# Attention and two expert layers on one core: both shared engines' work given to VectorE, the coarse attention regrouped, its v summed by DMA

## The chip, the cores and the metric

The kernel runs on 1 core of one Trainium2 chip. The metric is the device time of the whole program in microseconds (us). The kernel before takes 828.25 us in the median of 3 runs (823.25 to 828.64). The engines are PE (matrix products), DVE (VectorE), ACT (ScalarE) and POOL (GpSimd); SP issues the DMA transfers.

## The reference

For 4 batches, 8 heads, 576 positions and 64 columns, two attentions are added. The coarse one works on means of 4 neighbouring positions (144 of them): every position of a group gets its group's output. The local one lets a query see the keys less than 4 positions away. The sum passes two expert layers.

```
q_d, k_d, v_d = means over 4 neighbours          # 144 x 64 per head
out_up    = repeat(softmax(scale * q_d @ k_d.T) @ v_d, 4)
out_local = softmax(mask(scale * q @ k.T)) @ v   # |i - j| < 4
x = out_up + out_local                           # 2304 tokens x 512
x = ((x @ w1) * (x @ w2)) @ w3 @ w_out           # layer A, width 1024
x = max(x @ m1, x @ m2, x @ m3) @ m_out          # layer B, width 768
```

The weights are float64 in memory.

## The kernel before, in words

The core runs one stream of tasks per engine. The functions add tasks to a `Program` (`add`), each with its engine or engines, an estimate of its cost there, the tiles that it reads and writes, and for a DMA its size. `order` plans the tasks forwards and backwards six times, keeps the best plan, and writes the instructions out in its order; every engine then works through its own list in order and waits by semaphores. A task with two options (`either`: DVE or POOL) goes to the one that the planner thinks ends it first. So the cost table (lines 305 to 310) and the lags between engines (`AFTER`, `lag`) set the order.

The work, with the names that the profile shows:

- **Weights.** Each block of 128 x 1024 float64 words (`raw`) becomes float32 in five steps (`float32`, lines 358 to 364): one on ACT, then four on DVE, which this document calls a conversion. The conversions of `wo` and `w3t` give `wf` (12 blocks); w3 and w_out are then multiplied on PE into one matrix (`pw`, line 591, in two halves of 32 products each in the program, 64 in all; the trace shows each product as two matmuls). The 8 blocks of w1, w2 and the 12 of layer B give `cv`, and each is split into a high half (ACT, line 334) and a low half (`w`, an `either` task, line 336). A product in layer A or B is three matmuls on such halves (`mm3`, lines 341 to 343).
- **Coarse attention**, `down`, 16 pairs of heads (4 per batch; "head" below means such a pair). `qk` is loaded, copied into planes for the local attention (ACT, line 392), and summed in fours (lines 397 and 399, `either`). Scores `sp` on PE: 3 windows of 64 queries, six products (line 408); maximum (DVE, 418), exponentials with sums (ACT, 423), 4 x sum (POOL, 429), reciprocal (DVE, 431), multiplication (line 432, `either`), transposes `pp` (PE, 440), copies (ACT, 443), products with v `po` (PE, 456). v is loaded whole (`vr`, one buffer, line 387) and summed in fours by two additions (447 and 449, `either`).
- **Local attention**, `slab`, 12 slabs of 192 queries: scores `sq` (PE, 501), mask, maximum, exponential, sum and division on DVE and ACT (508 to 520), transposes `ptq` (526), products `poq` (543), sum with the coarse output (DVE, 552), split into halves `xt` (ACT 334, `either` 336).
- **Layers A and B**: 6 chunks of 384 tokens, two slabs each; `front` (products `pf` with x or `yt`, combined into `z` on DVE, line 620, split into `g`), `back` (products `py`). Layer A begins when both slabs of chunk 0 and its first weights are there. Its output goes through memory (`y_dram`, `y`) to layer B. All A and B products stand in one fixed chain on PE.

Memory for weights is 12 slots; `raw` blocks, `wf` and split weights take turns in them. Four of the eight PSUM banks hold the long sums, four take everything else.

Of the kernel before, what the change touches and what calls it, by code (L numbers as in the profile page):

```python
# [16 lines left out]
P = 128  # L17
# [84 lines left out]
class Program:  # L102
# [41 lines left out]
    def order(self, rounds=6):  # L144

        ts = self.tasks
        for t in ts:
            for d in t.deps:
                ts[d].nexts.append(t.n)
        for t in reversed(ts):  # L150
            t.late = min((ts[n].late - self.lag(t.options, n) for n in t.nexts), default=0.0)
            t.late -= min(c for _, c in t.options) + t.size / self.RATE
        best = None
        for _ in range(rounds):
            done, places = self.forward()
            end = max(t.end for _, _, t, _ in done)
            if best is None or end < best[0]:
                best = end, done, places
            self.backward(done)
        for x, slot in best[2]:  # L160
            x.slot = slot
        return [(t, e) for _, _, t, e in sorted(best[1], key=lambda d: d[:2])]

    def lag(self, options, n):

        (e, _), *more = options
        to = self.tasks[n].options
        return 0.0 if not more and len(to) == 1 and e == to[0][0] != "SP" else self.AFTER[e]

    def backward(self, done):  # L170
# [6 lines left out]
        for _ in ts:  # L177
# [16 lines left out]
            for d in t.deps:  # L194
                left[d] -= 1
                by[d] = min(by[d], t.late - self.lag([(on[d], 0)], n))
                if not left[d]:
                    can[on[d]].append(d)

    def forward(self):  # L200
# [26 lines left out]
        while len(done) < len(ts):  # L227
# [30 lines left out]
            t.end = end + self.AFTER[e]  # L258
# [5 lines left out]
            for m in t.nexts:  # L264
                left[m] -= 1
                ready[m] = max(ready[m], end + self.lag([(e, 0)], m))
                if not left[m]:
                    offer(ts[m])
# [4 lines left out]
def attention_moe_kernel(ctx, tc, q0, k0, v0, mask0, ql, kl, vl, mask, qkp, vp, w12, w3t, wo, m123, mo, out):  # L273
# [20 lines left out]
    tqr, kr, qr, vwr, vrr, vdr = ring("tq", 2), ring("k", 5), ring("q", 5), ring("vw", 2), ring("vr", 1), ring("vd", 2)  # L294
# [10 lines left out]
    act = lambda n: [("ACT", 0.19 + n * 0.00085)]  # L305
    dve = lambda n: [("DVE", 0.16 + n * 0.00104)]
    psum = lambda n: [("DVE", 0.15 + n * 0.00104)]
    quick = lambda n: [("DVE", 0.12 + n * 0.0006)]
    either = lambda n: [("DVE", 0.18 + n * 0.00115), ("POOL", 0.2 + n * 0.0024)]
# [71 lines left out]
    def down(b, hp):  # L381
# [4 lines left out]
        v = vrr.tile([KH, 2, 4 * P], F32, "vr")  # L386
        dma(lambda: v(), lambda: vp[rd, i].rearrange("r p n -> p r n"), [], [v], KH * 4096 * 2)
# [3 lines left out]
        for to, x in ((lambda: w()[:, :S], 0), (lambda: k()[:, W:W + S], GD)):  # L391
            prog.add(act(S), lambda e, to=to, x=x: e.copy(
# [3 lines left out]
        s, vd = qk, vdr.tile([KH, 2, P], F32, "vd")  # L396
# [5 lines left out]
        sp = bank("sp")  # L402

        def scores(e):
            for w in range(QT):
                for a in range(2):
                    h = slice(a * D, (a + 1) * D)
                    e.matmul(  # L408
                        sp()[h, w * GD:(w + 1) * GD], s()[h, w * QS:w * QS + D], s()[h, GD:2 * GD],
                        start=True, stop=True,  # L410
# [3 lines left out]
        ex = er.tile([P, QT, GD], F32, "e")  # L414
        prog.add(pe(0.9), scores, [s], [sp, ex])
        two = twor.tile([P, 2, QT], F32, "two")
        spv = lambda: sp()[:, :QT * GD].rearrange("p (t n) -> p t n", t=QT)
        prog.add(psum(QT * GD), lambda e: e.reduce_max(two()[:, 0], spv(), axis=AX.X), [sp], [two])
        prog.add(act(3), lambda e: e.mul(two()[:, 0], two()[:, 0], -SCALE / 16.0), [], [two])

        def exponentials(e):
            for w in range(QT):
                e.activation(
                    ex()[:, w, :], spv()[:, w, :], AF.Exp, bias=two()[:, 0, w:w + 1], scale=SCALE / 16.0,
                    accum_out=two()[:, 1, w:w + 1],
                )

        prog.add([("ACT", 1.75)], exponentials, [sp], [ex, two])
# [3 lines left out]
        prog.add(either(QT * GD), lambda e: e.tensor_tensor(  # L432
            ex(), ex(), view(two(), QT, [[1, QT], [0, GD]]), op=ALU.mult), [two], [ex])
        pt = dpr.tile([KH, 2, 2, QT, QW], F32, "dp")
        for part in range(2):
            pp = bank("pp")

            def transposed(e, part=part, pp=pp):
                for w in range(QT):
                    e.transpose(pp()[:KH, w * P:(w + 1) * P], ex()[:, w, part * KH:(part + 1) * KH], ident)  # L440

            prog.add(pe(0.4), transposed, [ex], [pp, (pt, part)])
            prog.add(act(288), lambda e, part=part, pp=pp: e.copy(
                pt()[:, part].rearrange("p a t n -> p t a n"),
                view(pp()[:KH, :], 0, [[P + QW - QS, QT], [D, 2], [1, QW]]),
            ), [pp], [(pt, part)])
        prog.add(either(4 * P), lambda e: e.tensor_tensor(
            v()[:, 0], v()[:, 0], v()[:, 1], op=ALU.add), [], [v])
        prog.add(either(2 * P), lambda e: e.tensor_tensor(
            vd().rearrange("p h n -> p (h n)"), v()[:, 0, :2 * P], v()[:, 0, 2 * P:], op=ALU.add), [v], [vd])  # L450
        po = bank("po")

        def values(e):
            for a in range(2):
                for k in range(2):
                    e.matmul(
                        po()[a * D:(a + 1) * D, :GD], vd()[:, k, a * D:(a + 1) * D],
                        pt()[:, k, a].rearrange("p t n -> p (t n)"), start=(k == 0), stop=(k == 1),
# [5 lines left out]
        prog.add(pe(0.7), values, [vd, pt], [po, (od, hp)])  # L464
# [4 lines left out]
    def slab(n, xt, at):  # L469
# [36 lines left out]
        prog.add(pe(2.4), scores, [x for hp in range(HP) for x in planes[b, hp]], [*sps, st])  # L506
# [56 lines left out]
    def weights_product():  # L563
# [20 lines left out]
        for half in range(2):  # L584
            os = [Tile(b, [P, 512], F32, "pw") for b in acc]
            for n in range(NF):
# [6 lines left out]
                prog.add(pe(3.5), product, [dw, do], os, chained=True)  # L593
# [235 lines left out]
```

## Time and profile before

| what | value |
|---|---|
| median of 3 runs | 828.25 us |
| the profiled execution, its own time | 827.7 us |
| its span (first to last instruction) | 825.9 us |
| PE busy | 771.5 us, 93% |
| DVE, ACT, POOL busy | 399.7, 274.9, 138.6 us |

The profile is of one execution. Busy is the time in which an engine has an instruction running; PE is nearly always busy after the first 145 us, so the shares over the span say little of the beginning. The chain of waits that ended last is 75% PE and 11% DVE. In the views a row gives a group of instructions (line, engine, operation, output<-inputs, shapes, count, busy us, mean ns, idle time before them and what ended it) or, in the timeline, one instruction or a run of equal ones with its start and length.

### The profile page before, as it was taken

The page shows a single profiled execution, that of the slowest core. Times are in us where ns is not written, and L with a number is a line of the kernel's source. Part 1 is how long each engine was busy: PE and PEld are TensorE (multiplying, and loading weights), DVE is VectorE, ACT ScalarE, POOL GpSimd, SP SyncE. Part 2 cuts the span into 40 slices and gives each one's busy share as a digit, 9 for nine tenths or more (in the row PEclk, how much of TensorE's full clock was granted, in tenths as well). Part 3 has the DMA queues.
Part 4 walks back from the last instruction along what each step waited for, and adds up shares of the span by engine and source line. Part 5 has one row for each costly group of instructions (what it writes and reads, how often), then busy time and mean ns, then how long its engine had stood idle before and what let it go on. Part 6 is the DMA issues. An engine that isn't in the chain of part 4 may idle for free.

```text
span 825.9 us, 16670 instructions
## 1 busy us (share of the span) xinstructions
PE 771.5 (93%) x7120; PEld 711.2 (86%) x7120; DVE 399.7 (48%) x614; ACT 274.9 (33%) x585; POOL 138.6 (17%) x176
## 2 busy tenths in 40 slices
PE   2879877998999999999998999999999999999997
PEld 0334446998999989999998999899999999999997
DVE  5978999924143274254324599972222131311211
ACT  4255574331234443363212355422121121121111
POOL 2213479500001012010001026520000000000000
PEclk9999976999999999999999999999999999999999
DMA  9786553012103232221202377112101001010001
GB/s 336 230 309 202 160 176 77 15 49 60 39 4 77 67 103 56 77 72 26 60 6 89 121 240 252 61 44 87 39 1 39 1 1 39 1 39 0 20 20 39
DMA packets 45482, 68.85 MB, mean 83 GB/s; under 512 B 20640, under 2 KB 29856, under 8 KB 45408
## 3 DMA queue, kind: packets, MB, share of 16 engines
q1 hardware_dynamic: 45408, 67.79, 25.7%
q8 instruction: 56, 0.92, 0.5%
q14 instruction: 18, 0.15, 0.1%
HBM read 58.33 MB, written 9.44 MB: 82 GB/s over the span
## 4 chain that ended last, share of the span: by engine, by line
PE 75%; DVE 11%; DMA 7%; issue 4%; ACT 1%; POOL 1%; SPq 1%; ACTq 0%; POOLq 0%; DVEq 0%
PE pf L341 16%; PE pf L343 15%; PE pf L342 15%; PE py L341 7%; PE py L342 6%; PE py L343 6%; PE poq L543 3%; DVE cv L362 3%; DMA qk<-qkp 2%; PE pw L591 2%; DVE cv L364 2%; DMA vr<-vp 2%; PE sq L501 1%; DVE cv L360 1%; PE sp L408 1%
## 5 line engine op out<-in xcount | busy, mean ns | idle before, releaser
L620 DVE TENSOR_TENSOR z<-pf,z 128x384 f32<-128x384 f32 x120 | 66.7, 556 | 287.5 <-PE pf L343 287.2
L341 PE MATMUL pf<-yt,w 128*128 128x384 f32 x432 | 146.0, 338 | 1.4 <-DVE z L620 1.4
L343 PE MATMUL pf<-yt,w 128*128 128x384 f32 x432 | 145.9, 338 | 0.0
L342 PE MATMUL pf<-yt,w 128*128 128x384 f32 x432 | 145.9, 338 | 0.0
L341 PE MATMUL pf<-xt,w 128*128 128x384 f32 x384 | 134.3, 350 | 1.9 <-issue 1.1
L342 PE MATMUL pf<-xt,w 128*128 128x384 f32 x384 | 132.0, 344 | 2.1 <-POOL xt L336 2.1
L343 PE MATMUL pf<-xt,w 128*128 128x384 f32 x384 | 131.6, 343 | 0.0
L618 ACT COPY z<-pf 128x384 f32<-128x384 f32 x84 | 40.2, 479 | 168.2 <-PE pf L343 168.2
L334 ACT CAST g<-z 128x384 fp32r<-128x384 f32 x84 | 43.1, 513 | 149.4 <-DVE z L620 149.3
L591 PE MATMUL pw<-wf 128*128 128x512 f32 x128 | 66.1, 669 | 24.9 <-DVE wf L364 22.6
L341 PEld LDWEIGHTS pf<-yt,w 128*128 128x128 f32 x432 | 81.1, 188 | 2.0 <-issue 1.7
L342 PEld LDWEIGHTS pf<-yt,w 128*128 128x128 f32 x432 | 81.1, 188 | 0.0
L343 PEld LDWEIGHTS pf<-yt,w 128*128 128x128 f32 x432 | 81.1, 188 | 0.0
L341 PEld LDWEIGHTS pf<-xt,w 128*128 128x128 f32 x384 | 73.9, 192 | 4.7 <-issue 2.7
L591 PEld LDWEIGHTS pw<-wf 128*128 128x128 f32 x128 | 26.6, 216 | 57.8 <-issue 32.4
L342 PEld LDWEIGHTS pf<-xt,w 128*128 128x128 f32 x384 | 73.8, 192 | 2.6 <-POOL xt L336 2.6
L343 PEld LDWEIGHTS pf<-xt,w 128*128 128x128 f32 x384 | 73.7, 192 | 0.0
L341 PE MATMUL py<-g,wp 128*128 128x384 f32 x192 | 67.1, 350 | 0.4 <-ACT o L649 0.4
L342 PE MATMUL py<-g,wp 128*128 128x384 f32 x192 | 64.8, 338 | 2.1 <-issue 2.1
L343 PE MATMUL py<-g,wp 128*128 128x384 f32 x192 | 64.9, 338 | 0.0
L336 DVE TENSOR_TENSOR g<-z,g 128x384 fp32r<-128x384 f32 x72 | 42.2, 587 | 33.3 <-ACT g L334 33.0
L341 PE MATMUL py<-g,w 128*128 128x384 f32 x144 | 48.9, 340 | 1.9 <-ACT o L649 1.9
(90 smaller groups left out, 1118.2 us busy)
## 6 DMA issues: line engine op xcount, KB each, us to landing
qk<-qkp SPq DMA_DIRECT2D x16, 576.0 KB
raw<-m SPq DMA_DIRECT2D x18, 512.0 KB
raw<-w3t SPq DMA_DIRECT2D x16, 512.0 KB
raw<-w SPq DMA_DIRECT2D x16, 512.0 KB
vr<-vp SPq DMA_DIRECT2D x16, 288.0 KB
y_dram<-o SPq DMA_DIRECT2D x48, 96.0 KB
y<-y_dram SPq DMA_DIRECT2D x16, 288.0 KB
out<-o SPq DMA_DIRECT2D x24, 192.0 KB
```

The source lines that it names most:

```text
L334: prog.add(act(n), lambda e: e.copy(hi(), src()), reads, [(writes, ("hi", id(hi)))])
L336: psum(n) if from_psum else either(n), lambda e: e.tensor_tensor(lo(), src(), hi().bitcast(F32), op=ALU.subtract),
L341: nc.tensor.matmul(o, wlo, xhi, start=first, stop=False)
L342: nc.tensor.matmul(o, whi, xlo, start=False, stop=False)
L343: nc.tensor.matmul(o, whi, xhi, start=False, stop=last)
L360: prog.add(quick(1024), lambda e: e.tensor_scalar(u(), u(), 3, 0x3FFFFFF8, op0=ALU.logical_shift_left, op1=ALU.bitwise_and), [], [cv])
L362: prog.add(dve(1024), lambda e: e.scalar_tensor_tensor(u(), high(), 0xC0000000, u(), op0=ALU.bitwise_and, op1=ALU.bitwise_or), [raw], [cv])
L364: prog.add(dve(1024), lambda e: e.scalar_tensor_tensor(u(), low(), 29, u(), op0=ALU.logical_shift_right, op1=ALU.bitwise_or), [raw], [cv])
L543: e.matmul(pos[u]()[a * D:(a + 1) * D, i * BQ:(i + 1) * BQ], vw()[h, a, i], pt().rearrange("p a n -> p (a n)")[h, c:c + BQ], start=True, s ...
L591: e.matmul(os[i](), w()[:, i * P:(i + 1) * P], o(), start=n == 0, stop=n == NF - 1)
L618: prog.add(act(T), lambda e, pp=pp: e.copy(z(), pp()[:, :T]), [pp], [z])
L620: prog.add(psum(T), lambda e, pp=pp: e.tensor_tensor(z(), pp()[:, :T], z(), op=ALU.mult if kind == "A" else ALU.max), [pp], [z])
```

## The change

- `either` and `psum` become the DVE cost: POOL is no option any more for the low halves, the sums of q and k, or anything else. POOL keeps small memsets and the 4 x sum.
- The coarse scores take two windows of 72 queries for each head of the pair (four products on 72 rows, in two banks) in place of three windows of 64. The maximum is two instructions of 72 x 288 in place of one of 128 x 432, the exponentials four in place of three, the transposes eight of 72 x 72 in place of six of 72 x 128.
- The multiplication by the reciprocal moves from DVE or POOL to ACT: four instructions of 72 x 144.
- v's sum: four transfers of 72 x 256 (72 KB) into one tile `vd`, the first by SP, three by POOL with `accum_op` add, each of which waits for the one before; the two additions and `vr` go. `vd` has three buffers in place of two.
- The planner's costs and lags are rewritten (a DMA that POOL issues counts SP's lag).

```diff
-            t.late = min((ts[n].late - self.lag(t.options, n) for n in t.nexts), default=0.0)
+            t.late = min((ts[n].late - self.lag(t, t.options, n) for n in t.nexts), default=0.0)
...
+        if task.size:
+            return self.AFTER["SP"]
...
-            t.end = end + self.AFTER[e]
+            t.end = end + self.AFTER["SP" if t.size else e]
...
-    tqr, kr, qr, vwr, vrr, vdr = ring("tq", 2), ring("k", 5), ring("q", 5), ring("vw", 2), ring("vr", 1), ring("vd", 2)
+    tqr, kr, qr, vwr, vdr = ring("tq", 2), ring("k", 5), ring("q", 5), ring("vw", 2), ring("vd", 3)
...
-    act = lambda n: [("ACT", 0.19 + n * 0.00085)]
+    act = lambda n: [("ACT", 0.14 + n * 0.00098)]
-    psum = lambda n: [("DVE", 0.15 + n * 0.00104)]
-    quick = lambda n: [("DVE", 0.12 + n * 0.0006)]
-    either = lambda n: [("DVE", 0.18 + n * 0.00115), ("POOL", 0.2 + n * 0.0024)]
+    psum = dve
+    quick = lambda n: [("DVE", 0.16 + n * 0.00052)]
+    either = dve
...
-        v = vrr.tile([KH, 2, 4 * P], F32, "vr")
-        dma(lambda: v(), lambda: vp[rd, i].rearrange("r p n -> p r n"), [], [v], KH * 4096 * 2)
+        vd = vdr.tile([KH, 2, P], F32, "vd")
+        for r in range(TG):
+            prog.add(
+                [("SP", 0.36) if r == 0 else ("POOL", 1.0)],
+                lambda e, r=r: e.dma_start(
+                    vd().rearrange("p h n -> p (h n)"), vp[rd, i, r // 2, :, r % 2 * 2 * P:(r % 2 + 1) * 2 * P],
+                    **({"accum_op": ALU.add} if r else {})),
+                [], [vd], size=KH * 1024)
         prog.add([("POOL", 0.12)], lambda e: e.memset(k()[:, :W], 0.0), [], [(k, 1)])
         prog.add([("POOL", 0.12)], lambda e: e.memset(k()[:, W + S:], 0.0), [], [(k, 2)])
         prog.add([("POOL", 0.12)], lambda e: e.memset(w()[:, S:], 0.0), [], [(w, 1)])
         for to, x in ((lambda: w()[:, :S], 0), (lambda: k()[:, W:W + S], GD)):
-            prog.add(act(S), lambda e, to=to, x=x: e.copy(
+            prog.add([("ACT", 1.23)], lambda e, to=to, x=x: e.copy(
                 to().rearrange("p (c g r) -> p c g r", c=NC, r=TG), view(qk(), x, [[1, NC], [NC, NJ * NG], [2 * GD, TG]])),
                 [qk], [(k if x else w, 0)])
-        s, vd = qk, vdr.tile([KH, 2, P], F32, "vd")
+        s = qk
         prog.add(either(4 * GD), lambda e: e.tensor_tensor(
             qk()[:, :4 * GD], qk()[:, :4 * GD], qk()[:, 4 * GD:], op=ALU.add), [], [qk])
         prog.add(either(2 * GD), lambda e: e.tensor_tensor(
             s()[:, :2 * GD], qk()[:, :2 * GD], qk()[:, 2 * GD:4 * GD], op=ALU.add), [], [s])
-        sp = bank("sp")
+        sps = [bank("sp") for _ in range(2)]
         def scores(e):
-            for w in range(QT):
+            for half in range(2):
                 for a in range(2):
                     h = slice(a * D, (a + 1) * D)
                     e.matmul(
-                        sp()[h, w * GD:(w + 1) * GD], s()[h, w * QS:w * QS + D], s()[h, GD:2 * GD],
-                        start=True, stop=True,
+                        sps[a]()[:KH, half * GD:(half + 1) * GD], s()[h, half * KH:(half + 1) * KH],
+                        s()[h, GD:2 * GD], start=True, stop=True,
                     )
-        ex = er.tile([P, QT, GD], F32, "e")
-        prog.add(pe(0.9), scores, [s], [sp, ex])
-        two = twor.tile([P, 2, QT], F32, "two")
-        spv = lambda: sp()[:, :QT * GD].rearrange("p (t n) -> p t n", t=QT)
-        prog.add(psum(QT * GD), lambda e: e.reduce_max(two()[:, 0], spv(), axis=AX.X), [sp], [two])
+        ex = er.tile([KH, 4, GD], F32, "e")
+        prog.add(pe(0.55), scores, [s], [*sps, ex])
+        two = twor.tile([KH, 2, 4], F32, "two")
+        for a in range(2):
+            prog.add(psum(2 * GD), lambda e, a=a: e.reduce_max(
+                two()[:, 0, 2 * a:2 * a + 2], sps[a]()[:KH, :2 * GD].rearrange("p (t n) -> p t n", t=2), axis=AX.X),
+                [sps[a]], [(two, a)])
         prog.add(act(3), lambda e: e.mul(two()[:, 0], two()[:, 0], -SCALE / 16.0), [], [two])
-        def exponentials(e):
-            for w in range(QT):
+        def exponentials(e, a):
+            for w in range(2 * a, 2 * a + 2):
                 e.activation(
-                    ex()[:, w, :], spv()[:, w, :], AF.Exp, bias=two()[:, 0, w:w + 1], scale=SCALE / 16.0,
-                    accum_out=two()[:, 1, w:w + 1],
+                    ex()[:, w, :], sps[a]()[:KH, w % 2 * GD:(w % 2 + 1) * GD], AF.Exp, bias=two()[:, 0, w:w + 1],
+                    scale=SCALE / 16.0, accum_out=two()[:, 1, w:w + 1],
                 )
-        prog.add([("ACT", 1.75)], exponentials, [sp], [ex, two])
+        for a in range(2):
+            prog.add([("ACT", 1.16)], lambda e, a=a: exponentials(e, a), [sps[a]], [ex, two])
         prog.add([("POOL", 0.25)], lambda e: e.tensor_scalar(
             two()[:, 1], two()[:, 1], 4.0, 4e-9, op0=ALU.mult, op1=ALU.add), [], [two])
         prog.add([("DVE", 0.17)], lambda e: e.reciprocal(two()[:, 1], two()[:, 1]), [], [two])
-        prog.add(either(QT * GD), lambda e: e.tensor_tensor(
-            ex(), ex(), view(two(), QT, [[1, QT], [0, GD]]), op=ALU.mult), [two], [ex])
-        pt = dpr.tile([KH, 2, 2, QT, QW], F32, "dp")
+        def normalise(e):
+            for w in range(4):
+                e.mul(ex()[:, w], ex()[:, w], two()[:, 1, w:w + 1])
+        prog.add([("ACT", 1.12)], normalise, [two], [ex])
+        pt = dpr.tile([KH, 2, 2, GD], F32, "dp")
         for part in range(2):
             pp = bank("pp")
             def transposed(e, part=part, pp=pp):
-                for w in range(QT):
-                    e.transpose(pp()[:KH, w * P:(w + 1) * P], ex()[:, w, part * KH:(part + 1) * KH], ident)
-            prog.add(pe(0.4), transposed, [ex], [pp, (pt, part)])
+                for w in range(4):
+                    e.transpose(pp()[:KH, w * KH:(w + 1) * KH], ex()[:, w, part * KH:(part + 1) * KH], ident[:KH, :KH])
+            prog.add(pe(0.35), transposed, [ex], [pp, (pt, part)])
             prog.add(act(288), lambda e, part=part, pp=pp: e.copy(
-                pt()[:, part].rearrange("p a t n -> p t a n"),
-                view(pp()[:KH, :], 0, [[P + QW - QS, QT], [D, 2], [1, QW]]),
-            ), [pp], [(pt, part)])
-        prog.add(either(4 * P), lambda e: e.tensor_tensor(
-            v()[:, 0], v()[:, 0], v()[:, 1], op=ALU.add), [], [v])
-        prog.add(either(2 * P), lambda e: e.tensor_tensor(
-            vd().rearrange("p h n -> p (h n)"), v()[:, 0, :2 * P], v()[:, 0, 2 * P:], op=ALU.add), [v], [vd])
+                pt()[:, part].rearrange("p a n -> p (a n)"), pp()[:KH, :2 * GD]), [pp], [(pt, part)])
         po = bank("po")
         def values(e):
...
-                        pt()[:, k, a].rearrange("p t n -> p (t n)"), start=(k == 0), stop=(k == 1),
+                        pt()[:, k, a], start=(k == 0), stop=(k == 1),
-        prog.add(pe(0.7), values, [vd, pt], [po, (od, hp)])
+        prog.add(pe(1.05), values, [vd, pt], [po, (od, hp)])
```

The planner makes a new order from this. On **DVE at the beginning of the program** (from the fifth `wf` block on; `two` is the coarse maximum and reciprocal) before:

```order
L418 TENSOR_REDUCE two<-sp 128x3
L364 SCALAR_TENSOR_TENSOR wf<-raw,wf 128x1024
L359 TENSOR_SCALAR wf<-wf 128x1024
L360 TENSOR_SCALAR wf<-wf 128x1024
L362 SCALAR_TENSOR_TENSOR wf<-raw,wf 128x1024
L431 RECIPROCAL two<-two 128x3
L364 SCALAR_TENSOR_TENSOR wf<-raw,wf 128x1024
L432 TENSOR_TENSOR e<-e,two 128x432
L449 TENSOR_TENSOR vd<-vr 72x256
L399 TENSOR_TENSOR qk<-qk 128x288
```

and now:

```order
L366 SCALAR_TENSOR_TENSOR wf<-raw,wf 128x1024
L405 TENSOR_TENSOR qk<-qk 128x576
L407 TENSOR_TENSOR qk<-qk 128x288
L366 SCALAR_TENSOR_TENSOR wf<-raw,wf 128x1024
L405 TENSOR_TENSOR qk<-qk 128x576
L407 TENSOR_TENSOR qk<-qk 128x288
L427 TENSOR_REDUCE two<-sp 72x2 x2
L361 TENSOR_SCALAR wf<-wf 128x1024
L362 TENSOR_SCALAR wf<-wf 128x1024
L364 SCALAR_TENSOR_TENSOR wf<-raw,wf 128x1024
L366 SCALAR_TENSOR_TENSOR wf<-raw,wf 128x1024
L443 RECIPROCAL two<-two 72x4
```

All sums of q and k now stand between the conversions on DVE; the multiplication (432) and the sum of v (449) are gone from it.

On **POOL after its first memsets** (numbers are buffers: `vd_155`, `vd_159`, `vd_161` belong to heads 1 to 3, `vd_526` and `vd_573` to heads 4 and 5) before:

```order
L397 TENSOR_TENSOR qk_145<-qk_145 128x576
L399 TENSOR_TENSOR qk_145<-qk_145 128x288
L429 TENSOR_SCALAR two_249<-two_249 128x3
L447 TENSOR_TENSOR vr_155<-vr_155 72x512
L397 TENSOR_TENSOR qk_153<-qk_153 128x576
L429 TENSOR_SCALAR two_325<-two_325 128x3
L432 TENSOR_TENSOR e_331<-e_331,two_325 128x432
```

and now, from the second head's `two` on:

```order
L441 TENSOR_SCALAR two_333<-two_333 72x4
L392 DMA vd_161<-vp 72x256
L392 DMA vd_155<-vp 72x256
L392 DMA vd_159<-vp 72x256
L392 DMA vd_161<-vp 72x256
L392 DMA vd_526<-vp 72x256
L441 TENSOR_SCALAR two_565<-two_565 72x4
L392 DMA vd_573<-vp 72x256
L392 DMA vd_526<-vp 72x256
L392 DMA vd_573<-vp 72x256
L392 DMA vd_526<-vp 72x256
```

The arithmetic is gone from POOL; accumulating transfers of two heads alternate in its list, and the second transfer of head 4 stands behind the first of head 5.

On **DVE where layer B's weights are converted** (`cv`, `w`) one block before:

```order
L620 TENSOR_TENSOR z<-pf,z 128x384
L359 TENSOR_SCALAR cv<-cv 128x1024
L336 TENSOR_TENSOR w<-cv,w 128x512
L360 TENSOR_SCALAR cv<-cv 128x1024
L362 SCALAR_TENSOR_TENSOR cv<-raw,cv 128x1024
L364 SCALAR_TENSOR_TENSOR cv<-raw,cv 128x1024
```

and now:

```order
L630 TENSOR_TENSOR z<-pf,z 128x384
L361 TENSOR_SCALAR cv<-cv 128x1024
L338 TENSOR_TENSOR w<-cv,w 128x512
L338 TENSOR_TENSOR g<-z,g 128x384
L338 TENSOR_TENSOR w<-cv,w 128x512
L362 TENSOR_SCALAR cv<-cv 128x1024
L364 SCALAR_TENSOR_TENSOR cv<-raw,cv 128x1024
L366 SCALAR_TENSOR_TENSOR cv<-raw,cv 128x1024
```

The second low half of each block and the low half of `g`, which POOL did in this stretch, stand on DVE.

## Rows read from the trace of the kernel before

**Rows 1.** The page's head, the engines' busy time, and DMA's busy tenths in 40 slices.

```profile
span 825.9 us, 16670 instructions
PE 771.5 (93%) x7120; PEld 711.2 (86%) x7120; DVE 399.7 (48%) x614; ACT 274.9 (33%) x585; POOL 138.6 (17%) x176
...
DMA  9786553012103232221202377112101001010001
```

**Rows 2.** Busy time by stretch (columns as its first line says, x instructions).

```profile
core 0: us, PE busy (x) PEld busy (x) DVE busy (x) ACT busy (x) POOL busy (x), PEclk, DMA share, GB/s
8.31:131.08 122.77, 93.25 (x1073) 49.87 (x1073) 110.44 (x132) 65.08 (x125) 51.04 (x51) 0.89 0.69 230
131.08:144.86 13.78, 11.58 (x48) 10.75 (x48) 13.64 (x14) 7.02 (x11) 11.71 (x8) 0.71 0.24 50
144.86:466.00 321.14, 315.12 (x4009) 300.89 (x4010) 134.72 (x263) 108.59 (x255) 35.52 (x58) 0.99 0.19 55
468.25:545.67 77.42, 73.72 (x414) 72.21 (x413) 72.34 (x76) 38.50 (x69) 33.89 (x23) 1.00 0.54 178
545.67:825.90 280.23, 275.57 (x1568) 275.24 (x1566) 68.56 (x132) 51.64 (x123) 2.73 (x4) 1.00 0.07 24
```

**Rows 3.** DVE timeline, a conversion while POOL is idle.

```profile
8.31 0.69 DVE L359 TENSOR_SCALAR wf<-wf 128x1024 f32<-128x1024 f32 x1 [8.31 <-ACT wf L358]
9.04 0.69 DVE L360 TENSOR_SCALAR wf<-wf 128x1024 uint32<-128x1024 uint32 x1
9.77 1.22 DVE L362 SCALAR_TENSOR_TENSOR wf<-raw,wf 128x1024 uint32<-128x1024 uint32 x1
11.03 1.23 DVE L364 SCALAR_TENSOR_TENSOR wf<-raw,wf 128x1024 uint32<-128x1024 uint32 x1
```

**Rows 4.** Timeline of POOL and DVE, two instructions that overlap.

```profile
19.09 1.48 POOL L397 TENSOR_TENSOR qk<-qk 128x576 f32<-128x576 f32 x1 [14.12 <-ACT k L392]
...
19.34 1.79 DVE L360 TENSOR_SCALAR wf<-wf 128x1024 uint32<-128x1024 uint32 x1
```

**Rows 5.** Groups by line and shape over the whole span.

```profile
L336 DVE TENSOR_TENSOR wp<-pw,wp 128x512 fp32r<-128x512 f32 x8 | 5.1, 674 | 0.0
...
L397 DVE TENSOR_TENSOR qk<-qk 128x576 f32<-128x576 f32 x9 | 6.8, 758 | 11.4 <-ACT k L392 11.4
...
L418 DVE TENSOR_REDUCE two<-sp 128x3 f32<-128x432 f32 x16 | 9.7, 603 | 14.9 <-PE sp L408 14.8
...
L508 DVE TENSOR_TENSOR s<-sq,masks 128x256 f32<-128x256 f32 x24 | 9.1, 416 | 13.2 <-PE sq L501 13.2
...
L423 ACT ACTIVATE e<-sp,two 128x144 f32<-128x144 f32 x48 | 17.7, 378 | 0.6
```

**Rows 6.** Timeline of POOL and PE where layer A begins.

```profile
133.72 1.98 POOL L336 TENSOR_TENSOR xt<-x,xt 128x384 fp32r<-128x384 f32 x1
...
131.08 0.69 PE L341 MATMUL pf<-xt,w 128*128 128x384 f32 x1 [0.66 <-DVE x L552]
...
133.16 0.52 PE L341 MATMUL pf<-xt,w 128*128 128x384 f32 x1
135.75 0.69 PE L342 MATMUL pf<-xt,w 128*128 128x384 f32 x1 [2.07 <-POOL xt L336]
```

**Rows 7.** PE timeline, one head's scores, 16 matmuls of the weights' product.

```profile
59.79 0.95 PE L408 MATMUL sp<-qk 64*64 64x144 f32 x12
61.01 7.13 PE L591 MATMUL pw<-wf 128*128 128x512 f32 x16 [0.27 <-DVE wp L336]
```

**Rows 8.** Two loads of v: the chain of waits, the SP queue, POOL's wait.

```profile
13.87 12.86 DMA vr<-vp
...
82.65 0.32 SPq L313 DMA_DIRECT2D vr<-vp  x1
...
86.32 1.26 POOL L447 TENSOR_TENSOR vr<-vr 72x512 f32<-72x512 f32 x1 [2.83 <-DMA vr<-vp]
```

**Rows 9.** What POOL did between 466 and 545 us, by line.

```profile
L336 POOL TENSOR_TENSOR w<-cv,w 128x512 fp32r<-128x512 f32 x11 | 19.1, 1750 | 37.2 <-DMA y<-y_dram 19.6 <-ACT w L334 17.6
```

More of the change, by code (lines that the diff above doesn't have):

```diff
@@ L162, in order, with lag @@
         return [(t, e) for _, _, t, e in sorted(best[1], key=lambda d: d[:2])]
-    def lag(self, options, n):
+    def lag(self, task, options, n):
         (e, _), *more = options
+        if task.size:
+            return self.AFTER["SP"]
         to = self.tasks[n].options
@@ L195, in backward @@
                 left[d] -= 1
-                by[d] = min(by[d], t.late - self.lag([(on[d], 0)], n))
+                by[d] = min(by[d], t.late - self.lag(ts[d], [(on[d], 0)], n))
                 if not left[d]:
@@ L265, in forward @@
                 left[m] -= 1
-                ready[m] = max(ready[m], end + self.lag([(e, 0)], m))
+                ready[m] = max(ready[m], end + self.lag(t, [(e, 0)], m))
                 if not left[m]:
@@ L504, in scores @@
                         )
-        prog.add(pe(2.4), scores, [x for hp in range(HP) for x in planes[b, hp]], [*sps, st])
+        prog.add(pe(1.55), scores, [x for hp in range(HP) for x in planes[b, hp]], [*sps, st])
         for a in range(2):
@@ L591, in product @@
                         e.matmul(os[i](), w()[:, i * P:(i + 1) * P], o(), start=n == 0, stop=n == NF - 1)
-                prog.add(pe(3.5), product, [dw, do], os, chained=True)
+                prog.add(pe(3.45), product, [dw, do], os, chained=True)
             for i in range(4):
```

## The prediction, on record before the changed kernel ran

> **What bounds the kernel now.** I read the page's head first, then busy time by stretch. PE is busy 771.5 of 825.9 us [rows 1], so what can be won is PE's idle time and PE's own work. By stretch [rows 2]: from 144.86 us to the end PE idles 6.0 us in 321, 3.7 in 77 and 4.7 in 280 (the last few are the tail). Before 131.08 us it is busy 93.25 of 122.77 us, and it has nothing at all to do in the first 8. The beginning is where time lies: some 30 us.
>
> What holds PE there? DVE: 110.44 us of 122.77 [rows 2]. Layer A's first products need the converted weights and the slabs' x, and both come out of DVE. But DVE does not work at its own pace. With POOL idle a conversion takes 0.69 + 0.69 + 1.22 + 1.23 = 3.83 us [rows 3]. The same second step took 1.79 us when it started 0.25 us behind an addition on POOL [rows 4]: POOL's ended at 20.57, DVE's at 21.13, 0.56 us later. So DVE waited for POOL and then ran. POOL computed for 51.04 us in this stretch [rows 2]. The reader is to see that the two engines, given half the list each, mostly take turns.
>
> The second place is 468 to 546 us: DVE is busy 72.34 of 77.42 us there, with POOL at 33.89 [rows 2]. PE loses only 3.7 us.
>
> **The change part by part, DVE in the beginning.** I count the new order's DVE list up to the last of the four low halves `xt` of chunk 0, and price it undisturbed:
> - 16 conversions at 3.83 [rows 3]: 61.3 us.
> - 15 low halves of weights (`w`, `wp`) at 0.674 [rows 5]: 10.1. Four `xt` of 384 columns, between the 0.416 of 256 columns and the 0.674 of 512 [rows 5]: 0.56 each, 2.2.
> - Six sums of q and k of 576 at 0.758, six of 288 at about 0.45 (between the 0.416 and the 0.603 of 432 columns) [rows 5]: 4.5 and 2.7.
> - Ten maxima of 288 columns, 0.45 as well: 4.5.
> - Six mask additions at 0.416, ten slab operations of 512 columns at 0.68, eight sums x of 192 columns at 0.35, below the 0.416 [rows 5]: 2.5 + 6.8 + 2.8.
> - Nine short ones (reciprocals and the like), each below 0.416 [rows 5]: 2.
>
> That is 99.4 us. Neighbours overlap: the 132 instructions of [rows 2] last 115.8 us if their groups are added up, and 110.44 are busy, 0.04 us each; for 139 instructions 5 us come off, so I take 94.5 (bounds 92 and 99). DVE starts at 8.31 [rows 3] as before, since the first loads are the same. It idled 122.77 - 110.44 = 12.3 us in the stretch [rows 2], mostly for scores of PE and for loads; I keep that whole. So x is ready at 8.3 + 94.5 + 12.3 = 115.1. In the kernel before the last `xt` needed ended on POOL at 133.72 + 1.98 = 135.7, and PE went on at 135.75 [rows 6]: **20.6 us earlier**. PE had done seven matmuls of layer A by then (131.08 to 133.16 is six of them, 0.35 each [rows 6]), which are 2.4 us that now come later: **18.2 us** won.
>
> **What covers the rest in the beginning.** PE's own work before layer A, 93 us with a clock of 0.89 of full speed [rows 2], begins with the second conversion at 16 us and would be done by 110 without a wait, so it is close behind DVE. ACT gets four multiplications, one exponential and its accumulator read more per head. If each costs the 0.378 of an exponential of 144 columns [rows 5], that is 2.3 us per head and 11 for five heads on top of 65.08 of 122.77 [rows 2]; ACT is free for 30 us even so. Cost zero; if that cover went, 2.3 us per head would. Behind the multiplication on ACT stand the next block's first conversion step and the copies of the transposes; it waits for the reciprocal on DVE, which waits for POOL's 4 x sum. SP issues as many loads as before; the bytes of v are the same. The scores take two of the four small banks in place of one: nothing, as long as PE has other products in them to wait behind.
>
> **The sum of v** is the change's new wait. Four transfers in a row make one `vd`, and the fourth head's first may start only when the first head's `po` has freed a buffer. No row shows an accumulating transfer. Bounds for one step: a whole load of v, four times as large, took 12.86 us in the beginning's full queue, and 86.32 - 82.97 = 3.4 us later on [rows 8]; the lower bound is nothing, if it lies beside others. I take 3.4, since the steps that matter run after 75 us, where DMA is busy 6, 5 and 5 tenths of a slice after 7 to 9 in the first three [rows 1]. In the new PE list the first `po` stands behind 48 of the 64 products of the weights. Their second half began at 61.01, at 7.13 us for 16 matmuls [rows 7]; 16 products are 32 matmuls, so 75. One head's work and 8 products later, at 85, comes the second `po`. POOL's list holds the fourth head's second accumulation behind the fifth head's first, which needs that `po`. From 85: a load of q and k ahead in the queue, 2.5; then three steps of 3.4; so v of head 4 at 98, and about 7 us from there to x (products, sum, halves, at the prices above): 105. That is hidden under 115.1 with 10 us to spare, or 3.3 us per step. So it costs zero up to 6.7 us per step, and it eats the whole gain at 85 + 2.5 + 3 steps + 7 = 135.7, at 13.7 us per step.
>
> **PE's work.** Scores: eight matmuls in place of 12 that took 0.95 [rows 7], 0.08 each: 0.3 us less per head. Transposes: more of them with fewer columns (576 against 768), between 0.2 less and 0.3 more: zero. Of the 16 heads six are scored before layer A, one less than before, so ten save 3.0 us later, and one head's work (scores, transposes, products, each at most 0.95) and one slab's scores move behind, +3.4. Net **+0.4**.
>
> **468 to 546 us.** The low halves of POOL come to DVE: a `w` costs 0.674 in place of 1.750 [rows 5, 9], a ratio of 0.39, so 33.89 us become about 13 (bounds 11 and 13, `g` and `yt` being shorter). DVE loses its stretching: 11 conversions at 3.83, 11 `w` at 0.67, 13 z and 4 `g` at 0.56 and some `yt` are 60 us where 72.34 were busy. Then 60 + 13 = 73 us: DVE stays as full as it was. PE's 3.7 us of idle [rows 2] may fall or stay; I take **-1** (bounds -3.7 and +5).
>
> **Sum**: 825.9 - 18.2 + 0.4 - 1 = 807.1 of span. The profiled execution took 827.7, 1.8 more than its span, so **809 us**; it lies 0.55 below the median of the runs, so against the median I expect 2.3% less.
>
> **The rivals.**
> 1. DVE's idle time shrinks as well, because part of it was waiting for POOL and for SP, which stood behind v's single buffer. Down to 4 us of 12.3: 8 us more, 801. For it: nothing in the new order makes DVE wait for POOL's arithmetic. Against it: PE's own 110 us.
> 2. The accumulating transfers are late. At 10 us per step v of head 4 comes at 117.5 and x at 124.5: 818.5; at 12.86 [rows 8] at 133: 827. For it: they queue among the blocks of weights, and POOL's 4 x sum, which the softmax of every head needs, stands in the same list. The Trainium skill, "SBUF — State Buffer", section "SBUF: two separate sides", says that POOL cannot write a transfer's descriptors while DVE runs in a mode with both ports, and gives 3.1 us in place of 0.62 for such a transfer. No row here shows one; by its 2.5 us more a step would be 5.9 us, just hidden, so it raises this rival and leaves the sum.
> 3. It gets slower: the long DVE instructions are not POOL's doing, or POOL's descriptors stretch them as its arithmetic did. Then the beginning wins nothing (the new list is as long as the old), and 468 to 546 gets POOL's 13 us on a DVE that is full: 825.9 + 0.4 + 13 + 1.8 = 841. It decides from about 9 us on that side with no gain at the beginning. Against it: [rows 3, 4], the same instruction at 0.69 and 1.79.
> 4. The new order is no better: another wait of PE in the beginning (a slab's softmax, a load) holds layer A at 131 or so. 824 to 830.
>
> **How the numbers follow.** My forecast (804 to 815) 0.60, rival 1 0.12, rival 2 0.16, rival 3 0.06, rival 4 0.06. This kernel's runs spread such that 1% (820 to 836.5) is about what can be told from no change. Faster by over 1%: 0.60 + 0.12 + 0.07 of rival 2 = 0.79; slower by over 1%: 0.05; the same: 0.16. The range from 797 to 823 leaves out rivals 3 and 4, the late half of 2 and the far end of 1.
>
> **What would show it.** Right: the second conversion step near 0.69 us throughout; layer A's first product at 110 to 118 us with no wait in it; POOL busy under 20 us of arithmetic; DVE in the conversion of layer B's weights still over 90% busy. Wrong: `po` waiting on a load of v, POOL's 4 x sum late behind a transfer, long conversion steps beside transfers of POOL, or PE waiting more than 5 us between the conversions of layer B's weights.

## The result, and the profile after

The changed kernel takes **803.82 us** in the median of 4 runs (800.64 to 806.30) against 827.21 for the kernel before (823.25 to 828.64): ratio 0.972, 95% interval 0.967 to 0.977. Another set gave 802.70 and 0.972 again (0.968 to 0.976, run x5). Forecast were 809 us and 797 to 823; the median lies just under the band of 804 to 815 that had the chance of 0.60, on the side of rival 1 (801). The profiled execution took 800.64 us, 798.8 of it span, and is the fastest of the four. Of the executions below, one of x9 took 1070 us at a granted clock of 0.65, and its median leaves that one out.

The page of after, answering to [rows 1]: PE's share is up from 93 to 95%, and POOL works 52.7 us in place of 138.6. Of these, 41.8 are the issuing of its 48 transfers; arithmetic and memsets are 10.9, where the prediction named under 20 as a sign.

```profile
span 798.8 us, 16686 instructions
PE 761.7 (95%) x7088; PEld 704.2 (88%) x7088; DVE 374.9 (47%) x676; ACT 300.1 (38%) x681; POOL 52.7 (7%) x130
```

By stretch, answering to [rows 2] (same columns). The first stretch ends with the last low half of x that layer A waits for, which came at 135.7 us before [rows 6]:

```profile
8.30:110.26 101.96, 86.69 (x905) 46.42 (x906) 93.16 (x139) 65.06 (x133) 21.68 (x37) 0.91 0.80 262
110.26:125.00 14.74, 9.66 (x39) 9.34 (x38) 9.08 (x13) 7.16 (x11) 3.86 (x4) 0.70 0.42 101
125.00:435.00 310.00, 306.92 (x4104) 290.45 (x4104) 134.36 (x285) 130.92 (x337) 23.51 (x56) 0.99 0.22 55
435.00:520.00 85.00, 85.00 (x486) 84.92 (x485) 71.38 (x102) 42.99 (x79) 0.00 (x0) 1.00 0.53 174
520.00:798.80 278.80, 273.39 (x1561) 273.07 (x1560) 66.92 (x142) 51.55 (x123) 0.00 (x0) 1.00 0.07 24
```

The reader is to see that x came 25.4 us earlier, that DVE needed 93.2 us of work for it, that PE lost 5.1 us right behind (second row, 9.66 of 14.74), and that PE has no gap at all where layer B's weights are converted.

The conversion steps of the 12 `wf` blocks in that first stretch (groups of DVE, mean ns of one). All stand at the undisturbed values of [rows 3], and so do those of the four `cv` blocks:

```profile
L364 DVE SCALAR_TENSOR_TENSOR wf<-raw,wf 128x1024 uint32<-128x1024 uint32 x12 | 14.7, 1225 | 0.4
L366 DVE SCALAR_TENSOR_TENSOR wf<-raw,wf 128x1024 uint32<-128x1024 uint32 x12 | 14.7, 1224 | 0.3
L362 DVE TENSOR_SCALAR wf<-wf 128x1024 uint32<-128x1024 uint32 x12 | 8.3, 693 | 0.3
L361 DVE TENSOR_SCALAR wf<-wf 128x1024 f32<-128x1024 f32 x12 | 8.2, 687 | 12.2 <-ACT wf L360 12.2
```

The same steps in the kernel before, from 8.3 us to its x at 135.7:

```profile
L364 DVE SCALAR_TENSOR_TENSOR wf<-raw,wf 128x1024 uint32<-128x1024 uint32 x12 | 16.2, 1354 | 0.3
L362 DVE SCALAR_TENSOR_TENSOR wf<-raw,wf 128x1024 uint32<-128x1024 uint32 x12 | 16.1, 1344 | 0.4
L362 DVE SCALAR_TENSOR_TENSOR cv<-raw,cv 128x1024 uint32<-128x1024 uint32 x6 | 11.4, 1895 | 0.1
L360 DVE TENSOR_SCALAR wf<-wf 128x1024 uint32<-128x1024 uint32 x12 | 10.0, 831 | 0.3
L359 DVE TENSOR_SCALAR wf<-wf 128x1024 f32<-128x1024 f32 x12 | 9.2, 770 | 8.9 <-ACT wf L358 8.8
L364 DVE SCALAR_TENSOR_TENSOR cv<-raw,cv 128x1024 uint32<-128x1024 uint32 x6 | 8.7, 1458 | 0.1
L360 DVE TENSOR_SCALAR cv<-cv 128x1024 uint32<-128x1024 uint32 x6 | 6.1, 1020 | 0.1
L359 DVE TENSOR_SCALAR cv<-cv 128x1024 f32<-128x1024 f32 x6 | 5.2, 860 | 0.0
```

Together they are 82.9 us for 18 conversions, where 16 take 61.3 now. At 3.83 us each, 14.0 of the 21.6 us between them are stretched steps, and 7.7 are two conversions that the new order puts behind x.

What PE waits for now (line, releaser: us in total, times, longest), then PE's timeline and ACT's, where the second of these waits comes from:

```profile
PE pw L601 <- DVE wf L366: 17.4, 2, 16.2
PE pf L343 <- ACT z L628: 5.1, 1, 5.1
PE pp L456 <- ACT e L447: 2.8, 1, 2.8
```

```profile
109.91 0.69 PE L343 MATMUL pf<-xt,w 128*128 128x384 f32 x1
...
118.47 0.69 PE L343 MATMUL pf<-xt,w 128*128 128x384 f32 x1 [5.08 <-ACT z L628]
```

```profile
116.86 1.19 ACT L400 COPY q<-qk 128x576 f32<-128x576 f32 x1 [4.73 <-DMA qk<-qkp]
117.94 0.48 ACT L628 COPY z<-pf 128x384 f32<-128x384 f32 x1
```

Layer A's first product starts at 109.91 us without a wait (131.08 before [rows 6]). Twelve matmuls later PE stops: the copy of `z` stands on ACT behind a copy of q, and that one waits for a load of q and k. Behind the wait, PE's matmuls start 0.32 us apart until 122.48 and 0.18 after that (the granted clock is 0.70 in the second row above), so some 2 us go on top of the 5.1. Nothing on PE waits for `vd`.

### The profile page after: what moved, and what is told of

Read it like the earlier page. It is cut to its first block, busy times and chain, and to the rows that moved or that the text cites. A ratio compares the mean times of both kernels' runs of the same rounds, so it can differ in the third digit from the quotient of the medians.

```text
span 798.8 us, 16686 instructions
## 1 busy us (share of the span) xinstructions
PE 761.7 (95%) x7088; PEld 704.2 (88%) x7088; DVE 374.9 (47%) x676; ACT 300.1 (38%) x681; POOL 52.7 (7%) x130
## 4 chain that ended last, share of the span: by engine, by line
PE 90%; DMA 4%; DVE 3%; ACT 1%; issue 1%; SPq 1%; ACTq 0%
PE pf L343 18%; PE pf L345 18%; PE pf L344 18%; PE py L343 8%; PE py L344 7%; PE py L345 7%; PE pw L601 4%; PE poq L553 3%; PE sq L511 2%; DMA raw<-wo 1%; PE po L466 1%; PE sp L417 1%; PE pp L456 1%; DMA vw<-v 1%; PE ptq L536 1%
## 5 line engine op out<-in xcount | busy, mean ns | idle before, releaser
L601 PE MATMUL pw<-wf 128*128 128x512 f32 x128 | 61.5, 635 | 17.6 <-DVE wf L366 17.4
L338 DVE TENSOR_TENSOR g<-z,g 128x384 fp32r<-128x384 f32 x84 | 46.7, 556 | 37.1 <-ACT g L336 37.0
L392 POOL DMA_DIRECT2D vd<-vp x48 | 41.8, 949 | 123.8 <-DMA vd<-vp 104.7
```

Of the source, the lines that this page charges most:

```text
L338: psum(n) if from_psum else either(n), lambda e: e.tensor_tensor(lo(), src(), hi().bitcast(F32), op=ALU.subtract),
L392: lambda e, r=r: e.dma_start(vd().rearrange("p h n -> p (h n)"), vp[rd, i, r // 2, :, r % 2 * 2 * P:(r % 2 + 1) * 2 * P], **({"accum_op": ...
L601: e.matmul(os[i](), w()[:, i * P:(i + 1) * P], o(), start=n == 0, stop=n == NF - 1)
```

## The experiments

In all of them "x" is the end of the last low half of x for chunk 0, and "DVE's list" what DVE worked from 8.3 us to there. Each ratio is against the kernel before in the same set of runs.

**x1: one line alone.** The kernel before, with POOL taken out of `either`:

```diff
-    either = lambda n: [("DVE", 0.18 + n * 0.00115), ("POOL", 0.2 + n * 0.0024)]
+    either = lambda n: [("DVE", 0.18 + n * 0.00115)]
```

> The kernel before with one edit: the low halves, the sums of q, k and v and the multiplication by the reciprocal have DVE as their only engine. Theory A (DVE waited for POOL's arithmetic): although DVE gets all of POOL's work, the conversions go back to 0.69 + 0.69 + 1.22 + 1.23 us, DVE's list before layer A is about 103 us (the 94.5 of the changed kernel, 3.6 for six multiplications, 6.7 for six sums of v, less 1.7 for the maxima), x is ready at about 124 us and the time is 814 to 819 us, half of the gain. Rival B (the gain is the regrouped attention, the sum of v by DMA and the work taken off DVE): nothing is taken off here, DVE gets some 19 us more at the beginning, 835 us or more. Rival C (the new order of the planner made it): 827.

805.23 us, ratio 0.973 (0.968 to 0.977): as much as the whole change. By stretch:

```profile
8.30:105.50 97.20, 80.37 (x886) 42.67 (x887) 92.60 (x135) 53.03 (x93) 2.55 (x16) 0.96 0.77 262
```

DVE's list is 92.6 us where 103 were expected, and DVE idles 4.6 where I had left 12.3 as they were, so the size was missed twice. The list is short because the planner makes another order: four heads' maxima stand ahead of x here, five in the changed kernel, seven in the kernel before. This one edit thus changes the order as well as the contention.

**x2: all but that line.** The changed kernel with the old `either`.

> The changed kernel with POOL as a second option again for the low halves and the sums of q and k, at the old costs. Theory A: the second conversion step is stretched again to 1.3 to 2 us beside POOL's additions, layer A begins 8 to 12 us later, 812 to 816 us. Rival B: nothing of the attention is undone, so the time stays at 804 or falls.

818.94 us, 0.990 (0.986 to 0.994), above the 812 to 816 expected, though layer A began only 5.2 us later (115.07) where 8 to 12 were expected. The 17 conversions ahead of x last some 71 us, of which 6 are stretched steps (14.0 in the kernel before). Another part of the loss lies elsewhere: behind a wait of 1.6 us for a copy of `z`, PE ran 13.7 us at a granted clock of 0.50, which by an estimate from that clock costs some 7 us.

```profile
292.00:305.70 13.70, 13.66 (x167) 12.37 (x168) 6.66 (x15) 3.57 (x8) 4.19 (x5) 0.50 0.25 44
```

By the medians the rest of the change gains 7 us beside POOL's option, and about nothing without it (x1). Each of these kernels has its own order, and how much of the 7 us is order or clock isn't shown.

**x3: the planner's new costs alone**, on the kernel before (`act`, `psum`, `quick`, and the two costs on PE).

> The kernel before with the new costs of ACT and DVE in the planner and of two PE tasks, nothing else; POOL keeps its option. Theory A: conversions stretched as before, 822 to 831 us. Rival C (the order): 805 to 815.

829.64 us, 1.006 (1.004 to 1.009). The costs bring nothing by themselves.

**x4: v summed on DVE again.** The changed kernel; `vp` is loaded whole, and two additions (72 x 512, 72 x 256) make `vd`, with one buffer each for v and `vd`.

> The changed kernel with v loaded whole by SP and summed by two additions on DVE again (one buffer each for v and its sum, for room). Theory A: six heads' additions of 0.69 + 0.42 put 6 to 7 us on DVE's list before layer A, 808 to 813 us. Rival D (the accumulating transfers cost time that the rest wins): 800 or less.

800.23 us, 0.969 (0.965 to 0.973), below the 808 to 813 expected. DVE's list didn't grow by 6 to 7 us: it is 90.2, since the planner puts four heads ahead of x, not five. The accumulating transfers win nothing over two additions of 1.1 us together; they lose nothing that can be told from zero either, each in its own order.

**x6: no accumulating transfers.** Only the first quarter of v is loaded, so the coarse output is that of a quarter of v; the tasks are gone from the plan too.

```diff
-        for r in range(TG):
+        for r in range(1):
```

> The changed kernel without the three accumulating transfers of each head: the coarse output is computed from the first quarter of v only, all else as it is. Theory A (those transfers are hidden, as 3.4 us per step under a slack of 10): 801 to 806, no difference. Rival D (the first products of layer A or POOL's small instructions wait for them): 4 us or more faster, 800 or less.

786.83 us, 0.954 (0.950 to 0.958): the rival's number, and a surprise. By stretch, and the DVE group that differs most by count (of `w`; 8 of them in the changed kernel; the `wp` are 4 in place of 8):

```profile
8.30:102.30 94.00, 80.31 (x883) 40.93 (x884) 86.98 (x131) 59.84 (x126) 4.51 (x17) 0.97 0.72 251
```

```profile
L338 DVE TENSOR_TENSOR w<-cv,w 128x512 fp32r<-128x512 f32 x6 | 4.0, 672 | 0.0
```

DVE's list before x is 6.2 us shorter than the changed kernel's 93.2: six low halves of weights and some work of a slab stand behind x here. That is another order, not a missing transfer. x9 and x10 part the two.

**x9: its own order, without the transfers.** The three tasks stay in the plan and issue nothing; every engine's list is the changed kernel's, without the three transfers. The coarse output is again that of a quarter of v.

```diff
-                lambda e, r=r: e.dma_start(
+                lambda e, r=r: None if r else e.dma_start(
...
```

> The changed kernel with its own order on every engine, instruction by instruction, but the three accumulating transfers of each head aren't issued (the coarse output uses the first quarter of v alone); nothing waits for them. Run x6 left them out of the plan as well, so that every engine's order changed, and came to 787 us; in its trace VectorE did 87.0 us of work before the last piece of x where the changed kernel does 93.2. Theory (x6 won by the order, not by the missing transfers): 797 to 804 us, with the wait of 5 us of the first layer-A products for the copy of z still there. Rival (the transfers themselves cost the 16 us, by landing late or by what they take from the other engines): 785 to 791 us.

798.3 us, 0.966 (0.962 to 0.970). As the theory said: in this order the transfers cost some 5 us by the two ratios, and as the interval meets that of the changed kernel, zero isn't ruled out. x6 is clear of x9: its order, both times without transfers, is worth some 10 us.

**x10: x6's order, with the transfers.** The planner is told that they cost nothing; PE's list is then the same as in x6, row by row.

```diff
-                [("SP", 0.36) if r == 0 else ("POOL", 1.0)],
+                [("SP", 0.36) if r == 0 else ("POOL", 0.05)],
...
-                [], [vd], size=KH * 1024)
+                [], [vd], size=0 if r else KH * 1024)
```

> The changed kernel with all its transfers, the accumulating ones too, but the planner is told that the three accumulating ones cost POOL 0.05 us and land at once: every engine's order is then that of x6, with the 72 accumulating transfers issued in it. Theory (x6 won by its order): 784 to 792 us, the first layer-A product at 98 to 104 us and no wait of it over 3 us. Rival (the transfers cost the 16 us): 798 to 808 us, with TensorE's products with v, or ScalarE's copies behind them, waiting for vd. Between the two, 792 to 798 us: the late landing costs a part of it in this order, which the planner no longer foresees.

824.89 us, 1.000 (0.997 to 1.003), above all that was expected, 38 us over x6. The longest waits of PE and of DVE, POOL's timeline, and PE's:

```profile
PE pp L456 <- ACT e L447: 35.8, 2, 24.0
...
DVE two L443 <- POOL two L441: 46.2, 6, 22.5
```

```profile
45.27 0.83 POOL L392 DMA_DIRECT2D vd<-vp  x1 [8.07 <-DMA vd<-vp]
51.99 1.69 POOL L392 DMA_DIRECT2D vd<-vp  x2 [5.90 <-DMA vd<-vp]
58.98 0.83 POOL L392 DMA_DIRECT2D vd<-vp  x1 [5.29 <-DMA vd<-vp]
61.73 0.83 POOL L392 DMA_DIRECT2D vd<-vp  x1 [1.92 <-DMA vd<-vp]
62.63 0.18 POOL L441 TENSOR_SCALAR two<-two 72x4 f32<-72x4 f32 x1
```

```profile
63.62 1.64 PE L456 MATMUL pp<-ident,e 72*72 72x72 f32 x8 [23.98 <-ACT e L447]
```

PE doesn't wait for `vd`. It waits for `e`: the sum 4x + eps stands in POOL's list behind nine transfers, each of which waits for the landing of the one before it of its head. The sum took 0.18 us and ran at 62.63; in x6 it ran at 37.23.

**x11: the same, and the small sum on DVE.** POOL's place for it in the plan stays and is empty, so PE's list is still that of x6.

```diff
-        prog.add([("POOL", 0.25)], lambda e: e.tensor_scalar(
-            two()[:, 1], two()[:, 1], 4.0, 4e-9, op0=ALU.mult, op1=ALU.add), [], [two])
-        prog.add([("DVE", 0.17)], lambda e: e.reciprocal(two()[:, 1], two()[:, 1]), [], [two])
+        prog.add([("POOL", 0.25)], lambda e: None, [], [two])
+        prog.add([("DVE", 0.17)], lambda e: (e.tensor_scalar(two()[:, 1], two()[:, 1], 4.0, 4e-9, op0=ALU.mult, op1=ALU.add),
+                                             e.reciprocal(two()[:, 1], two()[:, 1])), [], [two])
```

> Run x10 (all transfers, the planner told that the accumulating ones are free, the order of x6) with one thing more: the small sum 4x + eps of each head goes from POOL to VectorE, just ahead of the reciprocal; POOL's place for it in the plan is kept empty, so that TensorE's order is that of x6 and x10. POOL's queue then holds the accumulating transfers and the clearing of k and q alone. Theory (x10 lost its 38 us against x6 because the sums stood behind nine transfers in POOL's queue, each waiting for the landing of the one before: TensorE waited 35.8 us for e): 785 to 796 us, that wait under 5 us, faster than both kernels. Rival (the transfers are late for the products with v in this order, whatever POOL's queue holds): TensorE or ScalarE waits for vd instead, 800 to 825 us.

**791.26 us**, 0.958 (0.955 to 0.961): the best kernel of this study that does all the work, 1.4% under the changed one. The waits of PE, its stretch and layer A's start:

```profile
PE pw L601 <- DVE wf L366: 17.6, 2, 16.0
PE py L343 <- ACT o L659: 2.0, 3, 1.1
PE pp L456 <- ACT e L447: 1.9, 1, 1.9
```

```profile
8.30:102.30 94.00, 80.16 (x882) 40.71 (x882) 87.16 (x135) 59.54 (x124) 18.63 (x29) 0.97 0.82 262
```

```profile
99.98 0.69 PE L343 MATMUL pf<-xt,w 128*128 128x384 f32 x1 [0.25 <-ACT xt L336]
```

The 35.8 us are 1.9, and about 4 of x10's 38 us remain against x6.

**x7: a longer lag for DMA in the plan** (`"SP": 2.3` in place of 1.9), against the wait of 5.1 us for `z`.

> The changed kernel with 2.3 in place of 1.9 us as the planner's lag after a transfer. In the new order ACT's first copy of layer A's product then stands ahead of the copy of a q that is still loading. In the changed kernel PE waits 5.1 us for that copy and runs the following products at half pace until 122.5. Theory: the wait goes, 795 to 800 us. Rival E (another wait takes its place at the start of layer A, since x, weights and the next batch all come then): 803 to 806.

799.05 us, 0.967 (0.963 to 0.971). The wait for ACT's `z` is 0.6 us here, but PE waits 5.1 us for `e` in place of 2.8 and x comes at 113.8 us, 3.5 later. Its interval meets x5's, so the 3.6 us under x5 aren't settled; as the traces stand, one wait was traded for others.

**x8 and x12: POOL busy with work that nobody needs.** The changed kernel with 24 additions, or 80 memsets, of a scratch tile 128 x 512 in POOL's list at the beginning.

```diff
...
+    for _ in range(24):
+        prog.add([("POOL", 2.0)], lambda e: e.tensor_tensor(scratch, scratch, scratch, op=ALU.add))
```

> The changed kernel with 24 additions of 128 x 512 on a scratch tile put into POOL's list at the beginning, nothing depends on them. Theory A: POOL reads memory again, the conversion steps of the first 50 us are stretched to 1.2 to 2.3 us, layer A begins 8 to 15 us later, 812 to 819. Rival F (long conversion steps came from memory traffic of the loads, not from POOL): steps stay at 0.69 and 1.22, 804 to 806.

> The changed kernel with 80 POOL memsets of a scratch tile 128x512 at the beginning (0.53 us each in the trace of x8, 42 us in all, about what the 24 additions of x8 took with 37.9), which write and read nothing. Theory (any access of POOL to the memory stretches VectorE's conversion steps from 0.69 and 1.22 to 1.41 and 1.94 us, as in x8): 812 to 822 us. Rival (only instructions of POOL that read their operands, or read two of them, do it): 798 to 807 us, the steps at 0.69 and 1.22 beside the memsets.

x8 took 819.20 us, 0.992 (0.989 to 0.995); x12 813.76 us, 0.984 (0.981 to 0.988). One conversion of DVE beside POOL, and POOL's row over it, first of x8, then of x12 (timelines):

```profile
14.34 1.52 DVE L361 TENSOR_SCALAR wf<-wf 128x1024 f32<-128x1024 f32 x1
15.90 1.41 DVE L362 TENSOR_SCALAR wf<-wf 128x1024 uint32<-128x1024 uint32 x1
17.35 1.94 DVE L364 SCALAR_TENSOR_TENSOR wf<-raw,wf 128x1024 uint32<-128x1024 uint32 x1
19.32 1.95 DVE L366 SCALAR_TENSOR_TENSOR wf<-raw,wf 128x1024 uint32<-128x1024 uint32 x1
```

```profile
7.43 17.63 POOL L704 TENSOR_TENSOR scratch<-scratch 128x512 f32<-128x512 f32 x11
```

```profile
12.60 0.90 DVE L361 TENSOR_SCALAR wf<-wf 128x1024 f32<-128x1024 f32 x1
13.53 0.97 DVE L362 TENSOR_SCALAR wf<-wf 128x1024 uint32<-128x1024 uint32 x1
14.54 1.23 DVE L364 SCALAR_TENSOR_TENSOR wf<-raw,wf 128x1024 uint32<-128x1024 uint32 x1
15.80 1.23 DVE L366 SCALAR_TENSOR_TENSOR wf<-raw,wf 128x1024 uint32<-128x1024 uint32 x1
```

```profile
7.50 27.77 POOL L704 MEMSET scratch<- 128x512 f32 x39
```

Beside additions a conversion's steps take 6.82 us together in place of 3.83, and an addition 1.60 (17.63 over 11): some four additions for four steps, the engines taking turns. DVE's list grows from 93.2 to 110.3 us, layer A starts 16.5 us later (126.40), and x8 is 16.5 us over x5. DVE's idle time stays (8.2 us, 8.8 in the changed kernel) and none of it is a wait for POOL; PE's list is the changed kernel's row by row, and on DVE and ACT one step of one conversion changed places. So the contention is shown by itself. Beside memsets only the two steps with one input slow down. x12 confirms the size that the theory gave, but not its steps: of its 11 us over x5, the two steps make 6.2 (21 of them lengthened, most by 0.2 to 0.3; DVE's list is 99.5 us); elsewhere DVE waits 4.7 us for POOL's small sum, queued behind memsets.

## Why the prediction was right, point by point

- **POOL and DVE take turns: right.** The steps are at 0.69 and 1.22 throughout; x8 shows that POOL's arithmetic alone stretches them and moves layer A, and x1 that taking POOL out carries the gain. Rivals 3 and 4 fell. The gain holds a part of order too: of the 21.8 us that left DVE's list (115.0 before), 14.0 are stretched conversion steps and 7.7 two conversions moved behind x. What the second part is worth in time isn't shown.
- **DVE's list, 94.5 us: right** (93.2), and its start at 8.3 too. **"I keep that whole" of the 12.3 us of idle time failed**: DVE idled 8.8 in the changed kernel and 4.6 in x1. x came at 110.3, not 115.1. The size is half of rival 1's; its mechanism is shown in part. DVE waited 7.0 us for PE's scores and 1.3 for POOL in the kernel before; for scores it waited 1.9 in x1, where v's single buffer is still there, and 0.2 now. So doing away with that buffer wasn't needed for the fall; how the late scores hung on POOL isn't shown. For the conversions' first step on ACT it waits longer now, 3.9 us in place of 0.5.
- **ACT at zero: not quite.** PE waited once, 2.8 us, for a multiplication (`e`, L447), where it waited 1.2 us for one on DVE before. And ACT's list works in order, and a copy of q that waited for its load held `z`: 5.1 us of PE. The prediction looked at what stands behind the multiplication, and not at what stands behind a late load. x7 doesn't show that its removal alone pays.
- **The sum of v at zero: right in this order**, as far as x9 and x4 can tell. A step took 3.0 us from issue to landing in the median of all 48; the eleven between 79 and 108 us, the ones that the sum was about, took 2.6 to 4.7 (3.4 taken), and the nine before 60 us 3.1 to 8.8. The first `po` came at 71.26 and the second at 76.65 (75 and 85 taken). But what a transfer costs while hidden isn't all: the planner keeps room for it, and the order that it makes without them is some 10 us better (x6 against x9, both without transfers, 0.954 and 0.966; x11 has that order with them). And rival 2's "POOL's 4 x sum stands in the same list" was the real hazard: 38 us in x10.
- **PE's work and the rest.** The forecast of -18.8 us of span is -4.8 of PE's busy time (16 heads' scores at 0.3) and -14.0 of its idle time. Measured are -9.8 (771.5 to 761.7) and -17.3 (54.4 to 37.1). Idle time is the DVE point above. Of busy time, the scores gave 3.5 (16.0 to 12.5 us) and the transposes, priced at zero, 1.8 (14.1 to 12.3); the unforeseen part is the same 128 matmuls `pw`, 66.1 us before and 61.5 now, 669 and 635 ns apiece. Twenty of them took over 0.8 us before and ten now, most others 0.55 to 0.60. The granted clock was 0.89 over 122.8 us before layer A [rows 2] and 0.91 over 102 now, which fits: less of PE's work fell to the lower of the clock's two levels, 1.2 GHz.
- **Layer B's weights: right in direction**, at the bound: PE's 3.7 us of idle are 0 (taken 1). DVE's mark of over 90% held: from the first to the last conversion of these weights it is busy 68.04 of 73.24 us, 93%, as in the kernel before (72.34 of 77.42). The stretch of 85 us above begins 12 us earlier.

```profile
446.98:520.22 73.24, 73.24 (x419) 73.16 (x418) 68.04 (x94) 39.06 (x69) 0.00 (x0) 1.00 0.57 188
```

## What to carry to other kernels

Giving a share of one engine's elementwise work to a second engine can cost more than it brings where the two slow each other, as here: compare one instruction's duration alone and beside the other engine's before balancing a list by their separate costs. An engine that only issues waiting transfers still blocks what stands behind them, so small sums that a critical chain needs don't belong in that queue. Where a planner makes the order, separate the order from the operations (keep the one, drop the other) before a gain is put down to an operation.

## What the runs showed of the hardware

- POOL's reading additions lengthened each of the four conversion steps shown by 0.72 to 0.83 us (0.69 to 1.41 and 1.52, 1.22 to 1.94 and 1.95). That is less than such an addition takes by itself (the shortest of x8's took 1.04). POOL's memsets, which read nothing, lengthened only the steps with one input (0.69 to 0.90 and 0.97), and left those with two at 1.23. The Trainium skill, "SBUF — State Buffer", section "SBUF: two separate sides", tells it so: a VectorE operation with two inputs in SBUF collides only with a POOL operation that reads SBUF, one in a mode with both ports with any. x8 and x12 agree on the steps with two inputs; the steps with one input slowed beside both, but no run shows which mode they are in.
- POOL's accumulating transfers did not lengthen DVE's steps (693 and 1225 ns with them), and took 3.0 us from issue to landing in the median. The prediction's estimate from the same section of the Trainium skill, on descriptors, was a step of 5.9 us. The median is half of that; six of the nine steps before 60 us took 5.9 to 8.8. DMA's share was 1.03 from 40 to 60 us and 0.66 from 80 to 100, and no run tells a full queue from the rule.
